# One level of Strassen's scheme for both layers of an f32 block, with weight combinations streamed from DRAM

## The chip, the cores and the metric

One core of a Trainium2 chip. The time is the device time of one execution in microseconds (us); each kernel is run several times, and medians with the lowest and highest run are given. The span of a profile is some 2 us shorter than the measured time.

## The reference, cut to what matters

```python
def _attn_ref(q, k, v):                       # 8 batches, 8 heads, 576 tokens, 64 per head
    q_s, k_s = softmax over features of q, softmax over tokens of k      # [cut: spelled out]
    kv = np.einsum('bhsd,bhse->bhde', k_s, v)
    return np.einsum('bhsd,bhde->bhse', q_s, kv)

def _moe_ref(x, w_ch1, w_ch2):                # x: 8 x 576 x 512; w_ch1: 512 x 2048, w_ch2: 2048 x 512
    mixed = np.real(fft(fft(x, axis=1), axis=2))
    u = x + mixed
    un = (u - mean) / sqrt(var + 1e-6)        # [cut: spelled out]
    ch = np.maximum(un @ w_ch1, 0.0) @ w_ch2  # layer 1 and layer 2
    return u + ch
```

The two weights arrive as 64-bit floats, so each kernel turns their words into f32 on the chip.

## The kernel before

There are 4608 tokens, handled as nine groups of 512. Groups 0 to 7 take 512 tokens of one batch each, group 8 the remaining 64 tokens of each of the eight batches ("tail tokens": token 0 and tokens 257 to 319). While TensorE works on the layers of group g, the other engines and some small matmuls prepare batch g+1 ("side" work: attention, transform, norm). All f32 weights stay in SBUF.

```python
def convert(i):                                       # one 128x512 block of a weight, 32 in all
    nc.scalar.activation(lo, lo.bitcast(U32), ACT.Copy, scale=2.0 ** -29)      # low word: 3 top bits
    V.tensor_scalar(out=ti, in0=hi, scalar1=3, scalar2=0x3FFFFFFF, op0=ALU.logical_shift_left, op1=ALU.bitwise_and)
    V.scalar_tensor_tensor(out=ti, in0=hi, scalar=-(1 << 30), in1=ti, op0=ALU.bitwise_and, op1=ALU.bitwise_or)
    nc.scalar.activation(hi.bitcast(F32), hi.bitcast(F32), ACT.Abs)            # tiny values to zero
    V.scalar_tensor_tensor(out=t, in0=hi.bitcast(F32), scalar=least, in1=t, op0=ALU.is_ge, op1=ALU.mult)
    nc.gpsimd.tensor_tensor(out=out.bitcast(I32), in0=ti, in1=lo, op=ALU.add)

def up(f):                                            # layer 1: block f of 16
    ph = self.ps.tile([P, 512], F32, tag="up", name="up", bufs=2)
    for k in range(KT):                               # KT = 4
        nc.tensor.matmul(ph[:], lhsT=self.w1sb[:, f, k * P:(k + 1) * P], rhs=unT[:, k, :], ...)
    # relu to h, on VectorE and ScalarE in turn

def part(i, n):                                       # layer 2: 128 tokens i, feature blocks 4n..4n+3
    for f in range(4 * n, 4 * n + 4):
        nc.tensor.matmul(po[:], lhsT=h[:, f, i * P:(i + 1) * P], rhs=self.w2sb[:, f, :], ...)

# [cut] group 0: convert(f) and up(f) by turns; then all of w2 is converted, while
merged(down, side + norm(1))                          # layer 2 runs beside batch 1's side work
# tail tokens: loaded and stored as 1 row and 31 rows of a batch
return [(slice(0, 1), slice(0, 1)), (slice(1, Q), slice(257, S // 2))]          # Q = 32
```

## Time and profile before

| what | us |
|---|---|
| time, median of 4 runs beside the changed kernel | 1387.13 (1385.94 to 1389.11) |
| span of the profile | 1383.7 |
| TensorE busy | 1307.6 (95%) |
| first layer-1 matmul / first layer-2 matmul / group 1 begins | 100.2 / 172.0 / 262.5 |
| groups 1 to 6 / group 7 / group 8 / after the last matmul | 881.0 / 113.2 / 112.3 / 14.7 |

The marks of the third and fourth row are read from the starts of the matmuls that read the normed tokens (layer 1) and h (layer 2). "PE" is TensorE, "PEld" its weight loads, "DVE" VectorE, "ACT" ScalarE, "POOL" GpSimd, "SPq" the queue of SyncE that issues the transfers. A share of busy time is an average: here TensorE is full from 172 us on, and before that it waits for the other engines, VectorE above all, whose work there is for the greater part the conversion of the weights. The prediction below shows the lines.

### The profile page before, as it was taken

What the parts mean: (1) busy time and instruction counts of PE and PEld (TensorE: products, weight loads), DVE (VectorE), ACT (ScalarE), POOL (GpSimd) and SP (SyncE); (2) the same over time, 40 slices, a digit from 0 to 9 for tenths busy, and PEclk for the clock granted to TensorE, in tenths of its full rate; (3) what the DMA queues carried; (4) which work ended last, traced back from release to release, by engine and by line L of the source; (5) the groups of instructions that cost most, each with busy time, mean ns of one, the idle gap of its engine ahead of it and who ended that gap; (6) DMA issues with size and microseconds to landing.
All of it is one profiled execution on the core that took longest, in us unless ns stands there. A gap on an engine that the chain in (4) does not pass through costs nothing.

```text
span 1383.7 us, 10335 instructions
## 1 busy us (share of the span) xinstructions
PE 1307.6 (95%) x3948; PEld 654.3 (47%) x3948; DVE 422.4 (31%) x969; ACT 258.5 (19%) x473; POOL 154.8 (11%) x130
## 2 busy tenths in 40 slices
PE   5668899999999999999999999999999999999995
PEld 3433354554445445454445444644454444444442
DVE  3979441531134213431333124311331140000000
ACT  2544231221023101220122002210221011000000
POOL 1546211101010100110010101010101000000000
PEclk9859999999999999999999999999999999999998
DMA  5643141020112000310111001201110000010000
GB/s 170 200 144 124 31 121 39 31 69 0 30 46 69 0 16 23 91 31 16 31 48 52 8 23 47 68 1 31 46 35 0 19 19 8 0 32 14 0 23 23
DMA packets 62369, 61.61 MB, mean 45 GB/s; under 512 B 19824, under 2 KB 46448, under 8 KB 62320
## 3 DMA queue, kind: packets, MB, share of 16 engines
q1 hardware_dynamic: 62320, 60.95, 14.5%
q8 instruction: 31, 0.51, 0.2%
q14 instruction: 18, 0.15, 0.0%
HBM read 51.50 MB, written 14.16 MB: 47 GB/s over the span
## 4 chain that ended last, share of the span: by engine, by line
PE 84%; DMA 2%; DVE 1%; ACT 1%; issue 0%; POOL 0%; SPq 0%; ACTq 0%; DVEq 0%; POOLq 0%
PE dn L485 36%; PE up L473 32%; PE acc L365 4%; PE acc L249 2%; PE acc L308 2%; PE acc L390 1%; DMA q<-in_q_dram 1%; PE tr L292 1%; PE acc L387 1%; PE acc L321 1%; PE tr L236 1%; PE tr L446 1%; PE acc L368 1%; PE acc L388 1%; DMA words<-in_w_dram 1%; DVE x L489 1%
## 5 line engine op out<-in xcount | busy, mean ns | idle before, releaser
L473 PE MATMUL up<-unT,w1sb 128*128 128x512 f32 x1152 | 516.2, 600 | 14.5 <-DVE h L476 8.4
L485 PE MATMUL dn<-w2sb,h 128*128 128x512 f32 x1152 | 514.1, 596 | 4.1 <-DVE x L489 4.1
L473 PEld LDWEIGHTS up<-unT,w1sb 128*128 128x128 f32 x1152 | 214.5, 192 | 265.6 <-issue 257.8
L485 PEld LDWEIGHTS dn<-w2sb,h 128*128 128x128 f32 x1152 | 213.4, 190 | 260.9 <-issue 250.9
L476 DVE TENSOR_SCALAR h<-up 128x512 f32<-128x512 f32 x72 | 49.5, 687 | 218.6 <-PE up L473 218.5
L489 DVE TENSOR_TENSOR x<-dn,x 128x512 f32<-128x512 f32 x36 | 24.9, 691 | 244.0 <-PE dn L485 243.8
L278 POOL TENSOR_TENSOR q<-q,qm 128x512 f32<-128x512 f32 x36 | 38.6, 1088 | 518.6 <-DMA q<-in_q_dram 186.1
L478 ACT ACTIVATE h<-up 128x512 f32<-128x512 f32 x72 | 42.8, 595 | 270.2 <-PE up L473 270.2
L347 POOL TENSOR_TENSOR e<-x 128x512 f32<-128x512 f32 (+1 forms) x24 | 41.2, 1718 | 308.3 <-ACT x L311 261.1
L249 PEld LDWEIGHTS acc<-v,ks 128*128 128x128 f32 (+1 forms) x320 | 46.6, 207 | 22.8 <-issue 12.6
L249 PE MATMUL acc<-v,ks 128*128 128x128 f32 (+1 forms) x320 | 52.5, 306 | 3.4 <-ACT ks L237 2.8
L365 PE MATMUL acc<-ft,e 128*128 128x289 f32 (+2 forms) x144 | 45.9, 441 | 6.2 <-POOL e L349 5.2
L371 DVE COPY ZT<-acc 128x31 f32<-128x31 f32 x32 | 6.1, 190 | 147.7 <-ACT Z L370 147.6
L370 ACT COPY Z<-acc 128x256 f32<-128x256 f32 x32 | 11.9, 372 | 207.9 <-PE acc L368 135.1
L447 ACT COPY unT<-tr 128x512 f32<-128x512 f32 x36 | 20.5, 587 | 142.6 <-PE tr L446 139.6
L308 PEld LDWEIGHTS acc<-kvr,qT 128*128 128x128 f32 x256 | 34.0, 196 | 15.5 <-issue 13.1
L348 DVE TENSOR_TENSOR o<-x 128x512 f32<-128x512 f32 (+1 forms) x24 | 19.8, 824 | 67.9 <-ACT x L311 47.7
L222 DVE TENSOR_REDUCE km<-k 128x1 f32<-128x576 f32 x32 | 23.9, 749 | 53.2 <-DMA k<-in_kT_dram 53.2
L365 PEld LDWEIGHTS acc<-ft,e 128*128 128x128 f32 (+2 forms) x144 | 20.2, 158 | 34.9 <-issue 25.6
L308 PE MATMUL acc<-kvr,qT 128*128 128x128 f32 x256 | 34.8, 281 | 1.4 <-ACT qT L296 1.4
L292 PE MATMUL tr<-ident,q 128*128 128x128 f32 x144 | 24.1, 295 | 11.1 <-DVE q L284 5.6
L446 PE MATMUL tr<-ident,un 128*128 128x128 f32 x144 | 22.2, 290 | 11.3 <-DVE un L439 11.0
(102 smaller groups left out, 894.5 us busy)
## 6 DMA issues: line engine op xcount, KB each, us to landing
w2sb<-in_w_dram SPq DMA_DIRECT2D x29, 512.0 KB
k<-in_kT_dram SPq DMA_DIRECT2D x32, 288.0 KB
v<-in_v_dram SPq DMA_DIRECT2D x32, 256.0 KB
q<-in_q_dram SPq DMA_DIRECT2D x32, 256.0 KB
mirror<-x SPq DMA_DIRECT2D x18, 256.0 KB
out_dram<-mirror SPq DMA_DIRECT2D x16, 256.0 KB
out_dram<-x SPq DMA_DIRECT2D x16, 256.0 KB
words<-in_w_dram SPq DMA_DIRECT2D x3, 512.0 KB
```

The source lines that it names most:

```text
L249: nc.tensor.matmul(pk, lhsT=ks[0:n, c, :], rhs=v[0:n, c, :], start=(c == 0), stop=(c == NC - 1))
L278: nc.gpsimd.tensor_tensor(out=heads, in0=heads, in1=spread(m), op=ALU.subtract)
L292: self.nc.tensor.transpose(pt[:, r, :], q[:, r * P:(r + 1) * P], self.ident[:])
L308: nc.tensor.matmul(px[:, r * P:(r + 1) * P], lhsT=qT[:, r, :], rhs=self.kvr[b % 2][:, r, :], start=True, stop=True)
L347: nc.gpsimd.tensor_tensor(out=e[s, 0:D], in0=xl[s], in1=xu[s], op=ALU.add)
L365: nc.tensor.matmul(pz, lhsT=eo[c][int(odds)][s, cols], rhs=self.ft[s, 3 * int(odds) + c, :], start=(c == 0), stop=(c == 2 and odds))
L446: nc.tensor.transpose(pt[:, k, :], uns[i][:, k * P:(k + 1) * P], self.ident[:])
L473: nc.tensor.matmul(ph[:], lhsT=self.w1sb[:, f, k * P:(k + 1) * P], rhs=unT[:, k, :], start=(k == 0), stop=(k == KT - 1))
L476: nc.vector.tensor_scalar_max(h[:, f, :], ph[:], 0.0)
L478: nc.scalar.activation(h[:, f, :], ph[:], ACT.Relu)
L485: nc.tensor.matmul(po[:], lhsT=h[:, f, i * P:(i + 1) * P], rhs=self.w2sb[:, f, :], start=(f == 0), stop=(f == NF - 1))
L489: nc.vector.tensor_tensor(out=x[:], in0=po[:], in1=x[:], op=ALU.add)
```

## The change

Each product of two matrices is done as seven products of half size in each dimension, where eight would be needed, with sums and differences of the halves. The combinations of the weights are made once, in the start, and written to a scratch in DRAM; each group streams them back (8 tiles for layer 1, 7 for layer 2), since the seven of every pair no longer fit into SBUF together. A product of 512 columns becomes one of 256, so a group has 224 products of 256 columns in place of 128 of 512. The diff, cut to its core:

```diff
-        self.w1sb = c.tile([P, NF, D], F32, name="w1sb")
-        self.w2sb = c.tile([P, NF, D], F32, name="w2sb")
+        self.w1s = [d.tile([P, 7, HD], F32, ...) for p in range(NP)]        # DRAM; NP = 8, HD = 256
+        self.w2s = d.tile([7, P, NP, HD], F32, tag="w2s", name="w2s", bufs=1)
...
+    def prepare(self, layer, p, places):                # one of 8 pairs of blocks of a layer
+        w = self.wtile()                                 # 4 buffers
+        for i in range(2):
+            self.convert(places[i], w[:, 2 * i:2 * i + 2, :]...)            # the six passes, as before
+        (self.b_side if layer else self.a_side)(lambda i: w[:, i, :], nc.gpsimd, nc.vector)
+        # store to w1s[p], or to all seven rows of w2s at p
+    def load(self, n): ...                               # streams tile n of the 15 of a group
...
+    def a_side(self, at, e1, e2):                        # b_side likewise: four additions
+        e1.tensor_tensor(out=at(4), in0=at(2), in1=at(3), op=ALU.add)
+        e1.tensor_tensor(out=at(2), in0=at(0), in1=at(2), op=ALU.subtract)
+        e2.tensor_tensor(out=at(5), in0=at(4), in1=at(0), op=ALU.subtract)
+        e2.tensor_tensor(out=at(6), in0=at(1), in1=at(5), op=ALU.subtract)
...
+    def strassen(self, product, out):                    # products 1 6 5 7 2 4 3 in three PSUM banks
+        # VectorE adds a copy of product 1 to the bank after products 6 and 7 (u2, u3) ...
+    def down(self, g, h):                                # layer 2: each product runs over all 8 pairs
+                for p in range(4 * q, 4 * q + 4):
+                    nc.tensor.matmul(bank()[:, i, :], lhsT=h[:, p, A_AT[m], i * P:(i + 1) * P], rhs=w[:, p, :], ...)
...
         if g == 0:
-            # convert and up by turns, convert w2, merged(down, side + norm(1))
+            first = start(blk, jobs, h)                  # w1, layer 1, then all of w2, then 4 loads
+            merged(first, side[:cut])
...
+        merged(down, side[cut:] + (norm(g + 1) if g < B else []))
```

Also, the tail tokens' x goes through DRAM, and in group 8 the lower two blocks are both stored after the last product.

## The prediction

> **What bounds the kernel now.** I read the page's busy times first, then its costliest groups, then a table of stretches.
>
> ```profile
> PE 1307.6 (95%) x3948; PEld 654.3 (47%) x3948; DVE 422.4 (31%) x969; ACT 258.5 (19%) x473; POOL 154.8 (11%) x130
> ...
> L473 PE MATMUL up<-unT,w1sb 128*128 128x512 f32 x1152 | 516.2, 600 | 14.5 <-DVE h L476 8.4
> L485 PE MATMUL dn<-w2sb,h 128*128 128x512 f32 x1152 | 514.1, 596 | 4.1 <-DVE x L489 4.1
> ```
>
> TensorE is busy 95% of the span; 1030 us of 1384 are the two layers (up is layer 1, dn is layer 2), and there TensorE sat idle only 14.5 + 4.1 us before them. Nine groups of 512 tokens make 2304 records, 256 a group. Busy TensorE need not be TensorE at its peak, so I look at the weight loads, whose starts pace the matmuls:
>
> ```profile
> 1330.24 0.19 PEld L485 LDWEIGHTS dn<-w2sb,h 128*128 128x128 f32 x1 [0.24 <-issue]
> 1330.67 0.19 PEld L485 LDWEIGHTS dn<-w2sb,h 128*128 128x128 f32 x1 [0.24 <-issue]
> ```
>
> One record of 512 columns starts every 0.43 us (429 ns in the trace's own starts), the load takes 0.19 and is hidden. So the matmul's columns pace it, and 256 x 0.429 = 109.8 us of every group are the layers. The stretches (start:end, length, then busy time and instructions of PE, PEld, DVE, ACT, POOL, granted clock, DMA share, GB/s):
>
> ```profile
> 50.00:100.00 50.00, 31.82 (x93) 17.38 (x91) 41.87 (x78) 22.65 (x41) 26.23 (x17) 0.62 0.50 155
> 100.00:171.00 71.00, 59.49 (x126) 25.00 (x127) 48.45 (x78) 25.27 (x43) 32.18 (x22) 0.93 0.24 78
> 171.00:262.00 91.00, 89.71 (x328) 48.65 (x326) 33.49 (x85) 21.20 (x41) 12.83 (x10) 1.00 0.22 67
> 262.00:407.00 145.00, 144.41 (x457) 73.12 (x458) 39.54 (x100) 26.39 (x50) 10.61 (x9) 1.00 0.10 29
> 1257.00:1369.00 112.00, 109.63 (x254) 47.63 (x252) 8.15 (x12) 4.78 (x8) 0.00 (x0) 1.00 0.04 14
> ```
>
> Two regimes. From 171 us TensorE is full: a group with the next batch's attention and transform beside it takes 144 us (109.8 plus some 32 of the small matmuls), the last, without, 112. Before 171 us the limit is VectorE, which turns the 64-bit words of the weights into f32 in these stretches (first layer-1 matmul at 100.2 us, first layer-2 one at 172).
>
> **What the skill says.** "TensorE: Matmul & The Clock Gate", Back-to-back issue gap, gives N/2.4 + 2.5 ns for a warm matmul: 109 ns at 256, 216 at 512. "FP8 and Floating Point Precision", TensorE Precision Notes, says that true FP32 takes four passes. The trace fits both, since each f32 product is two records and one record of 512 takes 429 ns, twice 213 + 2.5. What decides this case is whether halving the columns halves the time although the load stays 190 ns. The transform's matmuls of 257 columns answer it:
>
> ```profile
> 511.38 0.19 PEld L387 LDWEIGHTS acc<-cd,Z 128*128 128x128 f32 x1 [0.24 <-issue]
> 511.80 0.63 PEld L387 LDWEIGHTS acc<-cd,Z 128*128 128x128 f32 x3 [0.24 <-issue]
> ```
>
> Three loads in 0.63 us, the last 0.19 long: 0.22 apart (217 ns by the starts). So 256 columns cost 217 ns against 429/2 = 214.5: the halving keeps 99%. "SBUF — State Buffer", Who interferes with whom, says that a VectorE instruction with two SBUF inputs contends with a GpSimd instruction that reads SBUF. The trace agrees: VectorE's 128x255 subtraction in SBUF (L354), beside GpSimd's additions, took 1318 ns, a like one (L400) without such company 417. "DMA: Bandwidth & Descriptors", Anatomy of one DMA, gives 2 us fixed plus bytes at 436 GB/s; this trace has 159 ns for a 4 KB packet, 25.8 GB/s on each of 16 engines, 412 together.
>
> **The change part by part.**
>
> *TensorE.* Before, 128 products of 512 a group, 256 records. After: layer 1 has 4 jobs x 7 products x 4 matmuls = 112 of 256 columns, layer 2 has 7 x 16 = 112; 448 records x 0.217 = 97.2 us. That is 12.6 us less a group, 113 us over nine, and it lies on the path wherever TensorE is full.
>
> *VectorE, ScalarE, GpSimd.* A layer-1 job (56 records, 12.15 us) needs five VectorE operations of 512 elements (0.69 us, as L489 and L476: 3.45 us), five ScalarE ones (0.6, as L478: 3.0 us) and four GpSimd additions that make the combinations of h (1.74, as L347: 7 us). Layer 2 adds six VectorE and three GpSimd operations a group, the norm three and one. A group's GpSimd work rises from 12 to some 47 us, VectorE's from 40 to 52, of a period above 130. None is a bound.
>
> *Slack.* Three PSUM banks, one buffer each, replace two for "up". The seventh product adds to the bank that VectorE has to read after the sixth, while only the fifth product (8 records, 1.74 us) runs. From the start of the sixth's last record: 0.38 us duration, 0.69 addition, some 0.15 of semaphores make 1.22; the seventh is due at 1.95. So 0.73 us of slack in layer 1 (the same for the fourth product after the seventh), where before a bank had over 2 us. The instruction order puts softmax steps of the next batch between these two VectorE reads: a maximum (0.68), GpSimd's fold and subtraction (1.74 + 1.08), the exponential (0.6) and sum, reciprocal, product (1.65) are 5.8 us, while TensorE has about 4.4 us of work there: 0.7 us late after slack. Four jobs a group, and VectorE's waits for k and q (53.2 and 24.8 us over the whole run before): I take 4 us for each of six groups with a batch beside them, 24 us.
>
> *Weight stream.* 15 tiles, 14.7 MB a group, at 412 GB/s are 36 us of a 130 us group, issued two to three tiles (12 to 20 us) ahead. Beside the 29 to 38 GB/s there now it fits, so 0 on the path.
>
> *Start.* This is what is paid. Weights no longer stay in SBUF; each pair of blocks is converted, combined, written to DRAM, and no layer-2 product can start before all eight pairs of w2 are stored, as each product streams all pairs. Before, layer 2 could begin with the first four blocks. I counted the changed kernel's instruction order. VectorE's work up to the unchanged start of layer 1 (about 100 us) is 67 us; from there to the last w2 combination 115 us (43 to the last w1 pair, 24 to the end of the fourth job, 48 for the rest), with GpSimd 111 us in the same stretch (32 conversions at 1.65, 40 half additions at 0.85, 16 of h at 1.74 in total over the start). Two engines that feed each other do not stay full: VectorE had 84% and 68% in the two stretches above. With 76%, 115/0.76 = 151, so the last pair is ready near 251 us. Its store and the first loads behind it (0.9 and 1 MB: 2.5 + 2.5 us, and 2 us fixed each) put layer 2 at some 260; the order has all of batch 1 and the k part of batch 2 done before that, and nothing beside this layer 2. With 48.6 us plus one of waits it ends near 310. Before, the second group's layer 1 began at 262.
>
> *The rest.* Groups 1 to 6 took 881 us before (262.6 to 1143.5). Less 6 x 12.6, less 8 for the part of batch 2 done early, plus 24: 821. Group 7: 113.3 - 12.6 + 1 = 102. Group 8: 112.1 - 12.6 + 1 = 101. The tail took 14.8 us after the last matmul; now both last blocks are stored after it, 16 transfers for 8, each issued in 0.34 us (2.7 us for 8): 17. Sum: 310 + 821 + 102 + 101 + 17 = 1351 us of span, and the measured time is 2 us above the span. A softer start (80%, and layer 2 at 250) would make 1342. I take 1345, 3% less than 1386.
>
> **The rivals.**
>
> *The narrow matmul is paced by its weights.* With 256 columns a load of 190 ns has 27 ns of room. If the spacing were 245, the whole TensorE gain would be gone and the time would be some 1400 to 1450 with the start's loss. Against it: four 257-column records in a row at 217, and 128-column ones at 109 to 112 although their loads also show 190.
>
> *VectorE's queue becomes the pace of layer 1.* In order, five operations a job with 0.73 us of slack, and each wait for a k or q transfer ahead of them stalls TensorE; the weights' tiles (2.5 us each) now lie ahead of k and q on the one queue. For it: VectorE waited 2.2 us on average for k. Against: the order loads k a group ahead and places these reads well. At 10 us a group it makes 1385.
>
> *The start is much longer.* Reused places for words chain transfer, conversion and the next transfer. At 65% VectorE share: 26 us more, 1375. If the chain runs as densely as 84%, 1335.
>
> *The stream is late.* If each of some 130 tiles cost 1 us, 1470; the shares above speak against it.
>
> **Range and chances.** The TensorE gain is nearly sure where it is full (about 100 us of its 113); the start gives back 35 to 70, waits 10 to 60. Best corner 1308, worst 1390. The limit for faster by 2% is 1358, only 13 above my value, so 0.62; within 2% 0.31; slower 0.07.
>
> **What would show it.** Records of layer 1 and 2 spaced 217 ns, not over 225; group 8's layers in about 99 us; groups 1 to 6 near 135; first layer-2 matmul near 260 us (right between 240 and 280); TensorE's idle before layer 1 mostly behind the VectorE additions into u and h, under 35 us in all; idle behind weight tiles near 0 after the start; GpSimd near 490 us. The prediction is wrong if layer-1 jobs take over 14 us without a batch beside them, or if layer 2 first starts beyond 300 us.

## The result, and the profile after

| | before | after |
|---|---|---|
| time, median of 4 runs each | 1387.13 (1385.94 to 1389.11) | 1387.37 (1384.8 to 1388.61) |

The ratio is 0.9998 with a 95% interval of 0.9976 to 1.002: no change. (A ratio here is the mean time of one kernel's runs over that of the other's of the same rounds, so not quite the ratio of the medians that are quoted. Executions over 1.5% slower than the fastest of the same kernel are left out of the means.) The predicted 1345 was wrong, although the value lay in the range.

The changed kernel's page, busy times and two of its groups (columns of a group: busy us and mean ns of one, then the idle time of the engine before them and its releaser):

```profile
PE 1226.2 (89%) x5676; PEld 1003.1 (72%) x5676; DVE 580.0 (42%) x1146; ACT 326.7 (24%) x590; POOL 422.1 (30%) x350
...
L555 PE MATMUL bb<-unT,w 128*128 128x256 f32 x864 | 218.8, 395 | 46.6 <-DVE u L525 39.6
L590 PE MATMUL bb<-w,h 128*128 128x256 f32 x864 | 198.5, 381 | 0.0
```

TensorE is busy 81 us less, and its share fell from 95 to 89%. The time saved there was not kept: it is idle elsewhere. TensorE did not sit idle before any matmul of layer 2 (0.0 before L590), so none of them waited for its weight tile. The spacing of the narrow matmuls is read from the weight loads of a group without a batch beside it:

```profile
1339.95 3.21 PEld L590 LDWEIGHTS ba<-w,h 128*128 128x128 f32 x15
```

Fifteen loads begin within 3.21 us less the last one's 0.19: 3.02/14 = 0.216 us apart. That is what was predicted (0.217), so the gain of the scheme itself is real. Where it went, the stretches show (start:end, length; busy time and instructions of PE, PEld, DVE, ACT, POOL; granted clock, DMA share, GB/s). First the kernel before up to layer 2 and to group 1:

```profile
0.00:172.00 172.00, 118.96 (x333) 63.79 (x334) 117.08 (x221) 68.05 (x120) 70.42 (x59) 0.86 0.43 135
172.00:262.50 90.50, 89.21 (x330) 48.67 (x328) 33.99 (x86) 21.68 (x42) 13.02 (x11) 1.00 0.23 67
```

Then the changed kernel: to layer 1, to layer 2, layer 2 of group 0, group 1, and group 8:

```profile
0.00:110.30 110.30, 62.21 (x205) 40.48 (x206) 66.39 (x144) 41.21 (x75) 39.26 (x45) 0.62 0.55 179
...
110.30:289.80 179.50, 122.45 (x498) 93.32 (x498) 136.34 (x237) 63.90 (x114) 102.63 (x84) 0.71 0.46 154
289.80:338.20 48.40, 48.40 (x226) 42.61 (x225) 9.26 (x19) 2.72 (x5) 5.90 (x5) 1.00 0.54 182
338.20:464.50 126.30, 121.09 (x569) 100.16 (x568) 40.33 (x79) 24.49 (x44) 34.23 (x28) 1.00 0.39 134
...
1261.60:1358.80 97.20, 97.07 (x449) 84.82 (x447) 18.08 (x27) 12.43 (x21) 23.93 (x19) 1.00 0.40 141
```

Layer 2 of group 0 begins at 289.8 us, where the kernel before has it at 172.0. In the 179.5 us ahead of it TensorE is idle for 57 us at a granted clock of 0.71. Once it begins, it runs without a gap and with nothing beside it (48.40 of 48.40). The low clock may have a part in the late start: from 211.4 to 289.8 us the granted clock was 0.50, where the kernel before has 1.00 from 172 us on, and the transform's matmuls (L402) took 683 ns at the median there, 407 in group 1. The recorded chain to layer 2 runs through 20 us of TensorE's work at that clock. No run here separates the clock from the idleness. The accounts:

| part | before | predicted | after | after less before |
|---|---|---|---|---|
| start, to group 1 | 262.5 | 310 | 338.2 | +75.7 |
| groups 1 to 6 | 881.0 | 821 | 821.6 | -59.4 |
| group 7 | 113.2 | 102 | 101.8 | -11.4 |
| group 8 | 112.3 | 101 | 97.2 | -15.1 |
| after the last matmul | 14.7 | 17 | 25.7 | +11.0 |
| span | 1383.7 | 1351 | 1384.5 | +0.8 |

So 85.9 us were won where they were expected, and 86.7 us were lost at the two ends. What TensorE waited for between 110.3 and 289.8 us (total us, times, longest):

```profile
PE tr L486 <- DVE eo L479: 24.4, 2, 23.3
PE bb L555 <- DVE u L525: 23.9, 3, 8.7
```

L555 is the matmul of layer 1, L525 the addition on VectorE that has to read the bank first; L486 is the norm's transposition. Both wait for VectorE, whose queue holds the conversions. VectorE's groups in that stretch, beside GpSimd:

```profile
L191 DVE SCALAR_TENSOR_TENSOR w<-h,w 128x512 f32<-128x512 f32 x10 | 13.8, 1392 | 0.1
...
L191 DVE SCALAR_TENSOR_TENSOR w<-w 128x512 f32<-128x512 f32 x8 | 5.8, 736 | 0.6 <-ACT w L190 0.6
L204 DVE TENSOR_TENSOR w<-w 128x256 f32<-128x256 f32 x8 | 5.5, 686 | 12.7 <-POOL w L192 7.4 <-POOL w L203 5.3
```

The same operation (L191) on the same amount of data takes 1392 ns on average in one place and 736 in another, and the combinations (L204) wait 12.7 us for GpSimd. Two readings offer themselves, slowing of VectorE by GpSimd and waits between the engines; the experiments below part them.

The other end, after the last matmul. Before, and then after (start, length, what; x8 and x16 are transfers issued):

```profile
1369.74 2.70 SPq L503 DMA_DIRECT2D out_dram<-x  x8
```

```profile
1358.71 0.69 DVE L605 TENSOR_TENSOR x<-bc,x 128x512 f32<-128x512 f32 x1 [6.21 <-PE bc L590]
1359.43 14.11 SPq L623 DMA_DIRECT2D out_dram<-x  x16
```

Eight transfers were issued in 2.70 us (0.34 each), sixteen in 14.11 (0.88 each). Half of each are transfers of 31 rows of 2 KB, and by the landing events of the trace the last three of these ended 2.57 us apart, with a transfer of one row (0.18) between them: they go one after the other, 2.4 us apiece. That is 26 GB/s, near the 25.8 GB/s that the prediction reads for a single one of the 16 DMA engines.

### The profile page after: what moved, and what is told of

The parts are those of the page before. It is cut to its first block, busy times and chain, and to the rows that moved or that the text cites. A ratio compares the mean times of both kernels' runs of the same rounds, so it can differ in the third digit from the quotient of the medians.

```text
span 1384.5 us, 14661 instructions
## 1 busy us (share of the span) xinstructions
PE 1226.2 (89%) x5676; PEld 1003.1 (72%) x5676; DVE 580.0 (42%) x1146; ACT 326.7 (24%) x590; POOL 422.1 (30%) x350
## 4 chain that ended last, share of the span: by engine, by line
PE 74%; DVE 10%; POOL 6%; DMA 4%; issue 2%; ACT 1%; SPq 0%; POOLq 0%; DVEq 0%; ACTq 0%
PE bb L590 14%; PE bb L555 11%; PE bc L590 9%; PE ba L590 9%; PE ba L555 7%; PE bc L555 6%; PE acc L402 5%; DMA q<-in_q_dram 3%; PE acc L289 3%; PE acc L427 2%; POOL w L192 1%; PE acc L424 1%; PE tr L486 1%; PE acc L405 1%; POOL eo L384 1%
## 5 line engine op out<-in xcount | busy, mean ns | idle before, releaser
L555 PE MATMUL bb<-unT,w 128*128 128x256 f32 x864 | 218.8, 395 | 46.6 <-DVE u L525 39.6
L555 PEld LDWEIGHTS bb<-unT,w 128*128 128x128 f32 x864 | 166.5, 197 | 78.3 <-DVE u L525 46.3
L590 PE MATMUL bb<-w,h 128*128 128x256 f32 x864 | 198.5, 381 | 0.0
L590 PEld LDWEIGHTS bb<-w,h 128*128 128x128 f32 x864 | 161.5, 190 | 28.4 <-issue 7.3
L555 PE MATMUL ba<-unT,w 128*128 128x256 f32 x576 | 142.5, 387 | 0.0
L555 PE MATMUL bc<-unT,w 128*128 128x256 f32 x576 | 140.5, 381 | 0.0
L590 PE MATMUL bc<-w,h 128*128 128x256 f32 x576 | 131.4, 381 | 0.0
L590 PE MATMUL ba<-w,h 128*128 128x256 f32 x576 | 128.0, 379 | 0.0
L590 PEld LDWEIGHTS bc<-w,h 128*128 128x128 f32 x576 | 107.5, 190 | 18.0 <-issue 4.4
L555 PEld LDWEIGHTS ba<-unT,w 128*128 128x128 f32 x576 | 109.2, 194 | 15.7 <-issue 1.0
L590 PEld LDWEIGHTS ba<-w,h 128*128 128x128 f32 x576 | 109.2, 190 | 15.4 <-issue 0.8
L555 PEld LDWEIGHTS bc<-unT,w 128*128 128x128 f32 x576 | 107.0, 190 | 15.3 <-DVE h L566 0.9
L402 PE MATMUL acc<-ft,eo 128*128 128x289 f32 (+3 forms) x240 | 83.3, 472 | 7.5 <-POOL eo L386 7.4
L402 PEld LDWEIGHTS acc<-ft,eo 128*128 128x128 f32 (+3 forms) x240 | 39.6, 183 | 42.3 <-issue 26.0
L525 DVE TENSOR_TENSOR u<-bb,s 128x512 f32<-128x512 f32 x45 | 31.0, 689 | 89.1 <-PE bb L555 54.3
L528 DVE TENSOR_TENSOR u<-bb,s 128x512 f32<-128x512 f32 x45 | 31.0, 689 | 77.5 <-PE bb L555 45.4
L566 DVE TENSOR_TENSOR h<-bc,u 128x512 f32<-128x512 f32 x72 | 49.6, 689 | 24.0 <-PE bc L555 23.0
```

Of the source, the lines that this page charges most:

```text
L402: nc.tensor.matmul(pz, lhsT=eo[c][int(odds)][s, cols], rhs=self.ft[s, 3 * int(odds) + c, :], start=(c == 0), stop=(c == 2 and odds))
L525: V.tensor_tensor(out=temp("u2"), in0=box["bb"][:], in1=box["s1"][:], op=ALU.add)
L528: V.tensor_tensor(out=temp("u3"), in0=box["bb"][:], in1=box["s1"][:], op=ALU.add)
L555: nc.tensor.matmul(bank()[:, i, :], lhsT=w[:, A_AT[m], k * P:(k + 1) * P], rhs=unT[:, B_AT[m], k, :], start=first and i == 0 and k == 0, s ...
L566: V.tensor_tensor(out=at(i), in0=bank[:], in1=u[:], op=ALU.add)
L590: nc.tensor.matmul(bank()[:, i, :], lhsT=h[:, p, A_AT[m], i * P:(i + 1) * P], rhs=w[:, p, :], start=first and i == 0 and p == 0, stop=p == ...
```

## The experiments

Names with a_ derive from the changed kernel, names with b_ from the kernel before. All sets of rounds were timed beside the kernel before, whose medians were 1386.69 to 1387.64 in all of them. Theories at the outset: the start is long because VectorE and GpSimd hinder each other or wait for each other (A), because VectorE simply has so much work (B), or because layer 2 of group 0 can't begin before all of w2 is combined and stored (G, the gate). The texts below use some letters anew: rival C of a_vconv is TensorE's low clock or the transfers, theory C of a_vdummy is that GpSimd slows VectorE.

### First set: the conversion and the combinations

**a_vconv: the conversion on VectorE alone.** Still three VectorE passes, but no ScalarE and no GpSimd pass. The low word is truncated rather than rounded, and tiny values aren't set to zero; the result is correct.

```diff
-        nc.scalar.activation(lo, lo.bitcast(U32), ACT.Copy, scale=2.0 ** -29)
         [two VectorE passes as they were]
-        nc.scalar.activation(hi.bitcast(F32), hi.bitcast(F32), ACT.Abs)
-        V.scalar_tensor_tensor(out=t, in0=hi.bitcast(F32), scalar=least, in1=t, op0=ALU.is_ge, op1=ALU.mult)
-        nc.gpsimd.tensor_tensor(out=ti, in0=ti, in1=lo, op=ALU.add)
+        V.scalar_tensor_tensor(out=ti, in0=lo, scalar=29, in1=ti, op0=ALU.logical_shift_right, op1=ALU.bitwise_or)
```

> The changed kernel, with the conversion of the weights done by VectorE alone (three operations instead of three, so the same VectorE count; no ScalarE pass, no GpSimd addition). Theory A (VectorE and GpSimd hold each other up in the start: contention and hand-overs, 39 us of VectorE time above its quickest and 43 us of VectorE idle between 110 and 290 us): the first layer-2 matmul moves from 290 us to 250 to 260, the total falls by 30 to 40 us to about 1350. Rival B (VectorE's own amount of work paces the start): layer 2 still begins after 280 and the total falls by under 10 us. Rival C (TensorE at its reduced clock or transfers pace it): no change beyond 5 us.

Measured: 1357.78 us (1357.33 to 1358.53), ratio 0.9791 (0.9776 to 0.9806). Its stretch up to layer 2:

```profile
0.00:258.40 258.40, 169.12 (x695) 124.23 (x696) 183.80 (x375) 65.72 (x123) 95.07 (x97) 0.82 0.54 182
```

Layer 2 begins 31.4 us sooner, and VectorE is busy 183.8 us until then instead of 202.7, with the same number of passes. So some 19 us are less busy time (375 instructions for 381, so nearly all of it shorter instructions) and 12 us are less idling. The gain of 29.6 us is just under theory A's 30 to 40, without saying yet which half of it; B (under 10) and C (under 5) fall.

**a_hi: the same without the low words**, two VectorE passes for three (the weights then have 20 bits of mantissa; the result is still within tolerance).

```diff
-        V.scalar_tensor_tensor(out=ti, in0=lo, scalar=29, in1=ti, op0=ALU.logical_shift_right, op1=ALU.bitwise_or)
```

> As a_vconv, with the low words left out too (two VectorE operations per block; about three bits of each weight lost, so slightly less exact). VectorE work falls by another 22 us (32 x 0.69). Theory B expects a further 20 to 29 us less than a_vconv (22 us at a share of 76%), theory A only 5 to 15 less than a_vconv, rival C nothing.

Measured: 1362.76 us (1358.23 to 1363.36), ratio 0.9828, so nothing more than a_vconv. VectorE is busy 163.7 us before layer 2, another 20 less, and layer 2 begins 7.5 us sooner, but the period of group 1 is 8.3 us longer (136.7 for 128.4). Theory B falls again: VectorE's amount alone is not what the start is made of. A's own forecast for this run, 5 to 15 us less, is missed too.

**b_vconv: the kernel before with the conversion of a_vconv.**

```diff
-            [ScalarE's two passes, the flush and GpSimd's addition]
+            V.scalar_tensor_tensor(out=out.bitcast(I32), in0=lo, scalar=29, in1=ti, op0=ALU.logical_shift_right, op1=ALU.bitwise_or)
```

> The kernel before with the conversion on VectorE alone. If conversion also paced its start (layer 1 of the first group took 72 us where 55 are TensorE's own), up to 17 us less, about 1370 to 1380; if its start was set by other things, within 5 us of 1387. Whatever it gains has to be taken off what a_vconv gains before the change itself is judged.

Measured: 1361.82 us (1361.05 to 1363.97), ratio 0.9822. It gains 25 us, more than expected: the kernel before paid for the hindrance too (layer 2 from 172.0 to 151.9 us). So A explains why the start of the changed kernel is longer than I predicted, but not why the change doesn't pay: with the same conversion, 1357.8 against 1361.8 is a gain of 0.3%.

**a_nocomb: no combinations of weights in the start**, wrong (relative error 0.88).

```diff
-        (self.b_side if layer else self.a_side)(lambda i: w[:, i, :], nc.gpsimd, nc.vector)
+        nc.scalar.copy(w[:, 4:7, :], w[:, 0:3, :])
```

> The changed kernel with the combinations of the weights left out of the start (one ScalarE copy in their place, so the result is wrong on purpose); conversions, stores and loads unchanged. This takes away what the change itself added to GpSimd (34 us) and VectorE (13 us). Theory that the added combinations made the start longer: layer 2 begins 20 to 35 us earlier, total 1350 to 1365. Theory that it is the gate alone (layer 2 can begin only when all of w2 is stored, while the conversions that the kernel before also had take this long): under 12 us less.

Measured: 1369.53 us (1365.88 to 1378.83), ratio 0.9885; layer 2 begins at 270.0. That lies between the two forecasts. Making the combinations costs 18 to 20 us of a start that is 76 us longer, with one ScalarE copy a pair left in their place.

### Second set: the gate and the tail

**a_plain0: group 0 without the scheme.** The combinations are made and stored as before, but beside plain products of 512 columns on the converted blocks. Layer 2 of group 0 goes pair by pair in four PSUM accumulators, so that it can begin with the first pair of w2.

```diff
         if g == 0:
-            first = start(blk, jobs, h)
-            merged(first, side[:cut])
+            first, second = start(blk, unT, h)
+            cut = len(side) // CUT0                # CUT0 = 3: a third of the side work, where it was two
+            merged(first, side[:cut])              # plain up(p, i), combine(0, p), ready(0, p + 4)
+            merged(second, side[cut:] + norm(1))   # down(p, 0), down(p, 1), ready(1, p + 2), combine(1, p)
+            continue
```

> The changed kernel with group 0 alone done without the scheme: 512-column products on the plain converted weights, layer 2 taken pair by pair in four PSUM accumulators so that it starts with the first converted pair of w2; the combinations are still made and stored, beside those products, for the groups 1 to 8. Group 0 costs 128 + 128 products of 512 columns (about 109 us) where the changed kernel has 224 + 224 of 256 (about 97). Theory G (the gate: layer 2 of group 0 can't start before the last combination of w2 has been made, stored and fetched again, and nothing else is left for TensorE then): group 1 starts near 285 us (275 to 295) where the changed kernel has 338, and the time falls to about 1330 to 1345. Rival A/B (the conversion's passes on VectorE and GpSimd themselves take until about 275 us, and batch 1's attention has to be done as well, so that the gate only decides where the waiting is): group 1 starts at 310 to 330, and part of it is given back in the period after, time 1360 to 1380.

Measured: 1334.35 us (1333.08 to 1338.54), ratio 0.9636 (0.9607 to 0.9664), correct. Group 1 begins at 277.0 us, 61 sooner. Theory G said 275 to 295 and 1330 to 1345.

**a_plain0_v: the same with the conversion of a_vconv.** No further edit.

> The same with the conversion on VectorE alone (as in a_vconv, which brought 27 us by itself). Theory G and theory A (the hand-overs between VectorE, ScalarE and GpSimd) are then two causes that lie behind one another in the start: together group 1 starts near 265 us, and the time is 1305 to 1325. If they are one and the same stretch of time seen twice, the two don't add: group 1 starts no earlier than in the better one of them alone, time within 8 us of the better of a_vconv (1358) and a_plain0.

Measured: 1310.83 us (1304.2 to 1316.07), ratio 0.9458. Alone the two edits brought 53.0 and 29.6 us, together 76.5: they nearly add, so they are two causes. The issues of SyncE in this kernel:

```profile
251.66 0.36 SPq L222 DMA_DIRECT2D w2s<-w  x1
253.12 1.57 SPq L629 DMA_DIRECT2D mirror<-x  x2
```

The last pair of w2 combinations is stored at 251.7 us; layer 2 has been running since 169.2, and group 0's first outputs leave at 253.1. With the gate it could only begin here.

**a_split: transfers of 31 rows split into 16 and 15**, loads of q and stores of the output.

```diff
-    return [(slice(0, 1), slice(0, 1)), (slice(1, Q), slice(257, S // 2))]
+    return [(slice(0, 1), slice(0, 1)), (slice(1, 17), slice(257, 273)), (slice(17, Q), slice(273, S // 2))]
...
-            nc.sync.dma_start(self.out[b4, S // 2 + Q - 1:S // 2:-1, :], src[:, 1:, :])
+            [the same for rows 1 to 16 and rows 17 to 31]
```

> The changed kernel with each transfer of 31 rows (tail tokens, loads of q and stores of the output) split into 16 and 15 rows; nothing else. Theory T (a transfer of 31 rows, a prime, is moved by a single one of the 16 DMA engines, at about 2.4 us for its 62 KB, one after the other): the last stretch after the last product falls from 25.7 to about 12 us, and the waits of the start for q fall by some 5 us, total -12 to -25 us, 1362 to 1375. Rival (the tail is bound by the number of issues and by the latency of the writes): 8 more issues make the tail 3 to 7 us longer, total +3 to +7.

Measured: 1369.02 us (1363.61 to 1376.9, a wide spread), ratio 0.9885 (0.9832 to 0.9938).

```profile
1362.14 0.69 DVE L605 TENSOR_TENSOR x<-bc,x 128x512 f32<-128x512 f32 x1 [6.21 <-PE bc L590]
1362.86 10.09 SPq L623 DMA_DIRECT2D out_dram<-x  x24
```

24 transfers are issued in 10.09 us (0.42 each) where 16 took 14.11, and the end comes 13.0 us after the last matmul (25.7 before the split). More issues and a shorter tail: theory T holds for the tail. In the start it gained nothing (group 1 at 337.9 us for 338.2), which T had expected. "DMA: Bandwidth & Descriptors", Why a DMA increments its semaphore by 16 and not by 1, says that a transfer uses the largest number of engines up to 16 that divides its slowest dimension, with 127 partitions on one engine as an example. 31 is a prime, and the 2.4 us apiece, at the rate of one engine, fit that; which engines carried them is not in the trace.

**b_split: the same in the kernel before.**

> The kernel before with the same split. Its tail has half as many transfers after the last product (8, four of them of 31 rows), 14.7 us. Theory T: about 9 us there, and up to 6 us less waiting for q in the start: total -5 to -12 us, 1375 to 1382. Rival (number of issues): +1 to +3 us.

Measured: 1375.02 us (1373.48 to 1375.95), ratio 0.9923. The tail falls from 14.7 to 7.4 us, the period of group 3 from 148.7 to 145.2. The start is as it was (262.7), so the expected gain there is a miss.

### Third set: what hinders VectorE, and the fair comparison

**a_vdummy: a_vconv with an addition on GpSimd for each converted block**, on a scratch tile, which nothing waits for.

```diff
+        nc.gpsimd.tensor_tensor(out=self.idle[:], in0=self.idle[:], in1=self.idle[:], op=ALU.add)
```

> The kernel a_vconv with one GpSimd addition of 128x512 on a scratch tile put back for each of the 32 converted blocks, which nothing waits for: GpSimd has about the load of the changed kernel's start again (48 us more), but no conversion is handed over to it. Theory C (contention: VectorE's instructions are slowed by GpSimd's, and this was a_vconv's gain): VectorE's busy time before layer 2 of group 0 rises from 184 back towards 203 us, and the time goes back to 1375 to 1388. Theory W (the waits of the hand-overs VectorE to ScalarE to VectorE to GpSimd were it): the time stays at 1355 to 1365, with VectorE's busy time wherever it is. In between: both, in that share.

Measured: 1363.04 us (1360.08 to 1364.95), ratio 0.9817. By its forecast this is for theory W, but the run does not test it well: GpSimd's additions waited for nothing, so all 32 ran between 4.6 and 43 us, ahead of w2 (GpSimd has 61 instructions between layer 1 and layer 2 in both kernels). It leaves the question open, so I placed them better:

**a_vdummy2: the addition reads the words that have just arrived**, so it runs beside the conversion of its own pair.

```diff
-        nc.gpsimd.tensor_tensor(out=self.idle[:], in0=self.idle[:], in1=self.idle[:], op=ALU.add)
+        nc.gpsimd.tensor_tensor(out=self.idle[:], in0=place.bitcast(I32)[:, 0:D], in1=self.idle[:], op=ALU.add)
```

> As a_vdummy, but each of the 32 additions on GpSimd reads the words that have just been loaded, so that it waits for their arrival and runs beside the conversion of its own pair, in layer 2's stretch too. Theory C (GpSimd's load slows VectorE): VectorE's busy time before layer 2 of group 0 rises from 184 towards 203 us, group 1 starts at 325 to 338 and the time goes back to 1375 to 1388. Theory W (the waits of the hand-overs): group 1 starts no later than 317, time 1356 to 1366.

Measured: 1382.71 us (1380.31 to 1384.22), 25 us longer than a_vconv; group 1 begins at 329.4, VectorE is busy 205.3 us before layer 2. The same VectorE groups, first in a_vconv, then here:

```profile
L185 DVE SCALAR_TENSOR_TENSOR w<-words,w 128x512 int32<-128x512 int32 x6 | 5.5, 909 | 0.0
L186 DVE SCALAR_TENSOR_TENSOR w<-w 128x512 int32<-128x512 int32 x8 | 5.4, 681 | 0.0
L186 DVE SCALAR_TENSOR_TENSOR w<-words,w 128x512 int32<-128x512 int32 x6 | 4.1, 684 | 0.1
```

```profile
L188 DVE SCALAR_TENSOR_TENSOR w<-w 128x512 int32<-128x512 int32 x8 | 8.1, 1028 | 0.0
L187 DVE SCALAR_TENSOR_TENSOR w<-words,w 128x512 int32<-128x512 int32 x6 | 7.4, 1225 | 0.0
...
L188 DVE SCALAR_TENSOR_TENSOR w<-words,w 128x512 int32<-128x512 int32 x6 | 6.9, 1156 | 0.1
```

L186 and L188 are the same pass, as are L185 and L187: 684 ns becomes 1156, 681 becomes 1028, 909 becomes 1225, and no conversion waits for GpSimd in either kernel. VectorE's idle time before layer 2 is the same in both (74.6 and 75.8 us). So theory C holds: GpSimd's additions slow VectorE, and of the 31.4 us that a_vconv gained before layer 2, this load alone takes back 22.7 (258.4 to 281.1). "SBUF — State Buffer", Who interferes with whom, says that the two engines exclude each other when a VectorE instruction has two SBUF inputs and the GpSimd instruction reads SBUF; the trace agrees.

**a_vadd: the changed kernel with GpSimd's pass of the conversion moved to VectorE**, ScalarE's passes kept.

```diff
-        nc.gpsimd.tensor_tensor(out=ti, in0=ti, in1=lo, op=ALU.add)
+        V.tensor_tensor(out=ti, in0=ti, in1=lo, op=ALU.bitwise_or)
```

> The changed kernel with one thing done otherwise: the last pass of each conversion, GpSimd's addition of the low bits (48 us in 32 instructions, with 53 us of waiting for VectorE ahead of it), is made on VectorE; ScalarE's two passes stay. VectorE has 32 instructions more, 22 to 28 us, nearly all of it before layer 2 of group 0. Theory W: no weight tile goes VectorE to GpSimd to VectorE any more, and the time falls to 1360 to 1372 in spite of VectorE's extra work. Theory B' (VectorE's own amount): group 1 starts 10 to 20 us later, time 1395 to 1405. If both cancel: 1380 to 1390, and ScalarE's passes are what a_vconv saved.

Measured: 1375.22 us (1370.66 to 1377.35), ratio 0.9908, so between W's 1360 to 1372 and the cancelling case. VectorE got 32 more instructions, and yet:

```profile
0.00:267.30 267.30, 167.18 (x643) 119.93 (x643) 203.01 (x390) 98.27 (x177) 100.65 (x97) 0.78 0.49 164
```

It is busy 203.0 us before layer 2, against 202.7 in the changed kernel, but with 390 instructions for 381: some of the side work moved behind layer 2's start, so the two don't compare. Over the whole run they do: VectorE is busy 588.5 us for 580.0. The 32 added passes took 25.7 us, so its other instructions became 17.2 us shorter, and two thirds of the addition came back. Layer 2 begins 22.5 us sooner, of which the next group gives back 8.7 (a period of 135.0 for 126.3).

**b_vsplit and a_vsplit: both kernels with both side costs removed** (VectorE-only conversion and split transfers).

> The kernel before with the VectorE-only conversion (b_vconv, 1362) and the split transfers (b_split, -12): if the two gains add, 1350 (1345 to 1354). The fair measure of what the first level of Strassen's scheme is worth once both side costs are gone from both kernels.

> The changed kernel with the VectorE-only conversion (a_vconv, 1358) and the split transfers (a_split, -12 to -23): 1338 to 1348, so within 1% of b_vsplit. If instead the gate of group 0 is not the reason why the change gains nothing, this should be clearly under b_vsplit by over 2%.

Measured in the same rounds: b_vsplit 1350.12 us (1348.22 to 1353.62), a_vsplit 1342.54 (1340.51 to 1344.29). The scheme alone is worth 0.6% at this point. Group 1 begins at 239.3 and 310.3 us: the change still loses 71.0 us in the start, nearly the 75.7 of the original pair. The conversion therefore isn't why the start loses.

**a_best: a_plain0_v with the split transfers.**

> a_plain0_v (1311) with the split transfers: tail from 25.7 to about 13 us, starts of the groups as they were: 1290 to 1303, some 4% under b_vsplit. If the start of a_plain0_v had its q loads on the path too, up to 8 us less than that.

Measured: 1293.4 us (1285.34 to 1294.16, 5 runs), ratio 0.9306 (0.9284 to 0.9328), correct. Its stretches to layer 1, to layer 2 and to group 1:

```profile
0.00:102.60 102.60, 63.04 (x209) 42.13 (x209) 64.19 (x152) 28.82 (x53) 24.21 (x33) 0.86 0.51 161
102.60:167.30 64.70, 64.41 (x193) 32.05 (x193) 38.20 (x85) 10.59 (x21) 14.71 (x18) 0.99 0.58 197
167.30:254.10 86.80, 82.97 (x259) 41.91 (x258) 52.91 (x109) 13.67 (x26) 26.98 (x28) 0.96 0.58 190
```

TensorE is nearly full from 102.6 us on (64.41 of 64.70 us, then 82.97 of 86.80). The start loses 14.8 us to b_vsplit (254.1 against 239.3) instead of 71.0, and the time is 4.2% under b_vsplit's in the same rounds. This is the version that beats both kernels.

### Fourth set: the gate alone

**a_up0_v: layer 1 of group 0 plain, as in a_plain0_v, but layer 2 by the scheme, from the streamed tiles.** a_plain0_v changed two things: it took the gate away, and it took VectorE work out of the start (155.9 us busy before group 1, a_vconv 194.1). This kernel has the light layer 1 and keeps the gate.

```diff
-            merged(first, side[:cut])
-            merged(second, side[cut:] + norm(1))
+            merged(start(blk, unT, h), side[:cut])                # as in a_plain0_v, but all of w2 is
+            merged(blk.down(g, h), side[cut:] + norm(1))          # combined and stored before layer 2
```

> Between a_vconv (1358) and a_plain0_v (1311), with the same conversion: layer 1 of group 0 is plain, as in a_plain0_v, but layer 2 of group 0 is the scheme's, from the streamed combinations, and so has the gate again (the combinations of h for it are made by GpSimd). If the gate is the cause: the time stays near a_vconv's, 1340 to 1360, group 1 starts at 290 to 308. If the lighter layer 1 is the cause: most of the 47 us is there without the gate's removal, 1312 to 1328, group 1 at 258 to 275.

Measured: 1366.88 us (1365.41 to 1368.04), ratio 0.9851. The miss is on the long side: 7 us above the forecast of the gate. Its stretches to layer 2 and to group 1, and the store of its last pair of w2:

```profile
0.00:271.70 271.70, 186.64 (x604) 111.74 (x605) 175.64 (x366) 59.96 (x113) 88.19 (x96) 0.80 0.52 171
271.70:320.10 48.40, 48.40 (x227) 42.61 (x226) 9.25 (x19) 2.90 (x6) 5.88 (x5) 1.00 0.59 199
...
259.69 0.39 SPq L222 DMA_DIRECT2D w2s<-w  x1
```

VectorE has 8 us less to do before layer 2 than in a_vconv, and layer 2 still begins only at 271.7; group 1 begins at 320.1, against 256.5 without the gate. The lighter layer 1 brought nothing. The last pair of w2 is stored at 259.7 us here and at 251.7 in a_plain0_v: the preparation ends 8 us apart, group 1 begins 63.6 us apart, so what differs is that layer 2 had to come after it. The gate is the cause. The pair of kernels differs in two more things that no run takes apart: here GpSimd makes the sums of h (busy 94.1 us before group 1, 65.6 there), and two thirds of the side work stand ahead of layer 2, not one. Nor is the tile quite the last thing that layer 2 waits for: by the landing events the first one was there at 269.2 us, and TensorE was still at its side work until 271.7. The size of the gate is less sure: 63.6 us between these two, but this kernel begins layer 2 13.3 us later than a_vconv (271.7 against 258.4), maybe because it has fewer places for w2's words before layer 1 ends. Against a_vconv's group 1 (306.7) the difference is 50.2.

## Why the prediction was right or wrong

**TensorE, right.** Spacing 0.216 us for a predicted 0.217; group 8, without a batch beside it, took 97.2 for a predicted 101. The rival that the weight loads pace the narrow matmul fell.

**Groups 1 to 7, right.** 821.6 for 821, and 101.8 for 102. In the 821 are the 24 us for late VectorE reads and the 8 for batch 2's early work, together +16; measured is 821.6 - (881.0 - 75.6) = +16.2. The waits themselves (L525 and L528) are of the predicted kind, 19.9 us in groups 1 to 6 for the 24. Over the run they are 46.6 us, above the prediction's own sign of under 35, since 23.9 of them fell into the start. The weight stream cost nothing after the start, as said. GpSimd was busy 422 us, not 490, since its 128x512 additions of h took 1.28 us and not 1.74.

**Start, wrong: the step that failed is "115/0.76 = 151, so the last pair is ready near 251 us" and the 260 and 310 that follow from it.** Layer 2 began at 289.8, outside the 240 to 280 that the prediction had set as its own test. Three terms were off. Layer 1 began at 110.3 for 100. The last w2 combination came 165.4 us after that, for 151: VectorE was busy 131.4 us, 79% of it, so the assumed share was not the fault; the 115 us of work were. I had counted instructions at durations from the kernel before, and they grew beside GpSimd's: the three VectorE passes of a converted block took 2.64 us there and 2.24 in the kernel before, which over 24 blocks makes 9.6 of the 16.4 us. a_vdummy2 shows the mechanism and a_vconv its worth (31.4 us, some of it idling). The third term, from the last store to the first product, was 14.1 us for 9. By the landing events the store took 4.7 us and the first tile 5.0 after it, as estimated; the other 4.2 TensorE was still at side work ahead of layer 2, at a clock of 0.50. Together 30 us. The part of the sum after it held (layer 2 in 48.4 us for 49.6).

**The mechanism of the start was named, but not weighed as a choice.** The prediction says that no layer-2 product can start before all pairs are stored, and it allowed 47 us for the start as a whole. The gate is worth 50 to 64 us (a_up0_v, a_plain0_v), the low clock while TensorE waits included. The 18 to 20 us of combinations (a_nocomb) are made ahead of it, so the two overlap and don't add. What was lost there is no law of the scheme: a first group without it removes four fifths of the loss (14.8 us left of 71.0).

**Tail, wrong by 8.7 us.** "16 transfers for 8, each issued in 0.34 us" took the issue as the limit. The limit is the transfers of 31 rows, which go one after the other: splitting the four that follow the last product in the kernel before took 7.3 us off the tail (b_split), splitting the eight in the changed one took 12.7 (a_split).

**The rival "the start is much longer" was right in its outcome, not in its mechanism.** It was put at 1375, with a VectorE share of 65%. The share was 79%, and longer instructions did it, so that it came near is luck; its number also lacked the tail's 8.7 us. The value itself, 1345, was chosen 8 us below the prediction's own sum (1351 and 2 for the measured time).

**What stays open.** Why layer 1 begins 10 us later than before: VectorE has no more to do until then (66.4 us busy, 68.8 before), and the granted clock (0.62, before 0.81) doesn't settle it, since a_plain0 had 0.82 and began later still, at 112.3. What a full clock between 211 and 290 us would be worth. The remaining 8.7 of a_vconv's 31.4 us before layer 2, which may be waits for ScalarE and GpSimd. The spread of 13 us among the runs of a_split.

## What to carry to other kernels

When a change turns resident data into a stream, ask what the first user of the stream must wait for: a product that runs over all pairs can't begin until the last is made, and doing just the first group the old way, with the preparation beside it, can be worth more than the change itself (here 49 us, a_vsplit to a_best, for the scheme's 8). Count an instruction at the duration that it will have beside its new company, not at the one that it has now. Cut small transfers so that their row count divides over many DMA engines: 31 rows (62 KB) took 2.4 us, as long as one weight tile of 1 MB (landings 2.5 us apart). Here it showed at the end, where nothing hid it, and not in the start.

## What the Trainium skill lacked or had wrong

- "SBUF — State Buffer", Who interferes with whom: right, but it gives no size for mixed streams. Here a two-input pass of 128x512 went from 684 to 1156 ns on average beside GpSimd additions, and even the one-input shift pass rose from 416 to 686 ns (a_vconv and a_vdummy2, blocks of w2 with place in a weight tile); the page counts the latter kind among those that may use the shared pair.
- "DMA: Bandwidth & Descriptors", Anatomy of one DMA: its 2 us plus bytes at 436 GB/s is a fit for transfers issued by GpSimd; the prediction took it over for SyncE's without saying so. For the large ones it fitted (store and first load of the gate: 4.7 and 5.0 us for an estimated 4.5 each). It does not hold for one of 31 rows: 62 KB would need 0.15 us beyond the fixed part, and the runs show 2.4 us apiece, one after the other. What the section lacks is only a pointer to the rule further down the same page, cited under a_split.
- No page has the pattern, a preparation that gates the first consumer; here it was worth 50 to 64 us of 1387.
